# Checking decoded weights: half of the second reads replaced by bytes kept while decoding, one bitwise pass per check, and w_out's sums moved

## Chip, cores and metric

One core of a Trainium2 chip. The metric is the device time of one execution in microseconds; three executions of the kernel before were timed. [...]

## What is computed

Attention with 4 sink keys and a window of 128 keys, then a two-layer MLP with a leaky ReLU, in float32 precision:

```python
def _attn_ref(q, k, v, n_sink, window):          # q, k, v: 4 x 8 x 768 x 64
    scores = scale * np.matmul(q, k.transpose(0, 1, 3, 2))
    keep = is_sink | in_window
    scores = np.where(keep, scores, -1000000000.0)
    a = np.exp(scores - np.max(scores, axis=-1, keepdims=True))
    a = a / (np.sum(a, axis=-1, keepdims=True) + 1e-09)
    return np.matmul(a, v)
...
    x = attn_out.transpose(0, 2, 1, 3).reshape(B * S, H * D)     # 3072 x 512
    h = x @ w_in                                  # 512 x 2048
    g = np.maximum(0.01 * h, h)
    return g @ w_out                              # 2048 x 512
```

The two weights arrive as 64-bit floats (`wq`, 32 blocks of 128 x 512 values, 512 KB each: 16 of w_in, 16 of w_out). The kernel has a general path for inputs with unusual limits or with weights out of a range of magnitude; a flag, computed at the end, says whether it has to run.

## The kernel before

The 3072 tokens are cut into eight units of 384. Units 0 to 5 go through the MLP by plain steps: `plain_step` takes one of 16 column blocks fc of w_in, makes h on TensorE (`h_part`, L420), the leaky ReLU on ScalarE and VectorE (L975, L981), and splits g into a high and a low part, both fp32r (`high_low`: ScalarE's cast L907, POOL's subtraction L908); `outputs` multiplies them with w_out (L927). All products are made from high and low parts in three passes. The last two units are multiplied together by a scheme of seven half-size products (`SEVEN`): eight `pair_step`s q make h (products z, L748), then `seven_outputs` makes the output (products y, L1254), 56 steps k. Attention of the next unit runs between the MLP steps (`soft`, `gather`, `values`, L442 to L604); `gather` transposes softmax rows (L506, L508), stores them to DRAM (`kd`, L510) and reads them back rearranged (`pt`, L512).

Weights. During unit 0, `fetch_weight` (L279) reads one block into one of three 512 KB buffers, `load_weight` decodes the two 32-bit words on VectorE (L291, L293, L295), `round_weight` splits the result (ScalarE L308, POOL L309). Checks: each of the 32 blocks is read a second time, from unit 2 on, by `fetch_check` (L327), and `check_weights` takes the largest and smallest magnitude of the top words with two VectorE reduces (L335). `check_step` is called at six column blocks of units 2 to 5 (`CHECK_AT`), then in pair steps 4 to 6 and at every third k of `seven_outputs`. `needs_general` reduces the two results to flags.

The seven products need sums of weight blocks. `prepare` does it for w_in, `prepare_o` for w_out (POOL: two sums L647, four passes of `sums` L656, two low parts L666 in `split_sums`, behind ScalarE's hio cast L665; the results go to DRAM, `tfar`). `hio` uses the same buffer (number 2) as many of the re-read blocks. Seven of the eight `prepare_o` start at the steps in `PREPARE_O`, the last in the pair stage. `conversions` does the same for the tokens (loads of `xfar` L702, POOL sums L704, casts L711, low parts L712). In a pair step `add` puts sums on VectorE or POOL by hand, `t2` and `t3` among them; `make` splits the pair's arrays for the output (all of these have line L1005 in the profile). `fetch_ts` reads `tfar` back.

Order. On TensorE the order is written by hand. On the other engines and on SP, which issues the transfers, a scheduler sets it from the program's order and its own estimates; each engine then works strictly in that order. `anchor` and `latest` tie an instruction to a place.

## Time and profile before

| | us |
|---|---|
| median of three runs | 673.57 (673.37 to 676.27) |
| profiled execution | 674.25 |
| its span, first to last instruction | 672.5 |
| TensorE busy, matmuls | 654.2 (97%) |
| TensorE busy, weight loads | 576.5 (86%) |
| VectorE busy | 493.5 (73%) |
| ScalarE busy | 344.3 (51%) |
| POOL busy | 517.8 (77%) |

Busy shares are averages over stages with different limits: unit 0 up to about 122 us with all the decoding, plain steps up to about 538 us, pair steps up to about 604 us, outputs to the end. A stage is read from the waits that TensorE has in it. Matmul ends are modelled in the profile, so an idle time of TensorE in a row can be some tenths of a us short. PE is TensorE, PEld its weight loads, DVE VectorE, ACT ScalarE.

### The profile page before, as it was taken

What the parts mean: (1) busy time and instruction counts of PE and PEld (TensorE: products, weight loads), DVE (VectorE), ACT (ScalarE), POOL (GpSimd) and SP (SyncE); (2) the same over time, 40 slices, a digit from 0 to 9 for tenths busy, and PEclk for the clock granted to TensorE, in tenths of its full rate; (3) what the DMA queues carried; (4) which work ended last, traced back from release to release, by engine and by line L of the source; (5) the groups of instructions that cost most, each with busy time, mean ns of one, the idle gap of its engine ahead of it and who ended that gap; (6) DMA issues with size and microseconds to landing.
All of it is one profiled execution on the core that took longest, in us unless ns stands there. A gap on an engine that the chain in (4) does not pass through costs nothing.

```text
span 672.5 us, 13091 instructions
## 1 busy us (share of the span) xinstructions
PE 654.2 (97%) x3884; PEld 576.5 (86%) x3884; DVE 493.5 (73%) x1327; ACT 344.3 (51%) x884; POOL 517.8 (77%) x625
## 2 busy tenths in 40 slices
...
GB/s 233 190 180 239 236 182 201 128 223 141 239 195 211 222 179 248 209 238 219 142 263 233 228 201 222 243 233 268 161 217 167 373 299 340 323 356 263 329 396 73
DMA packets 105964, 155.42 MB, mean 231 GB/s; under 512 B 23328, under 2 KB 69152, under 8 KB 105888
## 3 DMA queue, kind: packets, MB, share of 16 engines
...
## 4 chain that ended last, share of the span: by engine, by line
PE 81%; DMA 6%; DVE 5%; POOL 3%; issue 2%; SPq 1%; ACT 1%; DVEq 0%; POOLq 0%; ACTq 0%
PE h L420 25%; PE o L927 24%; PE z L748 9%; PE y L1254 8%; PE acc L573 5%; PE s L447 5%; PE s L442 2%; PE t L483 1%; DMA kd<-kt 1%; DMA odd<-tfar 1%; DMA work<-xfar 1%; DMA tfar<-owg 1%; POOL work L704 1%; PE warm L403 1%; DMA woraw<-in_wq 1%
## 5 line engine op out<-in xcount | busy, mean ns | idle before, releaser
L908 POOL TENSOR_TENSOR gl<-gmem,gh 128x384 fp32r<-128x384 f32 x91 | 93.6, 1029 | 49.4 <-PE o L927 37.7
L420 PE MATMUL h<-xmem,even 128*128 128x384 f32 x576 | 119.4, 342 | 1.0 <-DVE gmem L981 1.0
L420 PE MATMUL h<-xmem,odd 128*128 128x384 f32 x576 | 117.2, 340 | 0.5 <-DVE gmem L981 0.5
L456 ACT ACTIVATE pk<-pk,negm 128x132 f32<-128x132 f32 (+1 forms) x192 | 81.5, 425 | 64.9 <-DVE negm L454 60.5
L927 PE MATMUL o<-woh,gh 128*128 128x512 f32 x288 | 114.5, 398 | 0.0
L927 PE MATMUL o<-wol,gh 128*128 128x512 f32 x288 | 114.3, 397 | 0.0
L420 PEld LDWEIGHTS h<-xmem,even 128*128 128x128 f32 x576 | 99.5, 188 | 6.2 <-issue 1.9
L420 PEld LDWEIGHTS h<-xmem,odd 128*128 128x128 f32 x576 | 99.5, 188 | 5.6 <-issue 1.7
L927 PE MATMUL o<-woh,gl 128*128 128x512 f32 x288 | 85.3, 397 | 0.0
L907 ACT CAST gh<-gmem 128x384 fp32r<-128x384 f32 x96 | 49.0, 510 | 51.9 <-PE o L927 28.8
L393 POOL TENSOR_TENSOR qksp<-qkraw,qksp 64x396 fp32r<-64x396 f32 (+1 forms) x48 | 57.6, 1201 | 21.8 <-issue 11.7
L981 DVE TENSOR_TENSOR gmem<-h,gmem 128x384 f32<-128x384 f32 x95 | 52.3, 551 | 26.9 <-ACT gmem L975 26.2
L975 ACT ACTIVATE gmem<-h 128x384 f32<-128x384 f32 x95 | 46.2, 487 | 45.2 <-PE h L420 39.6
L454 DVE CUSTOM_DVE_ANT_0 pk<-s,m 128x132 f32<-128x132 f32 (+1 forms) x192 | 59.2, 317 | 8.9 <-PE s L447 3.6
L927 PEld LDWEIGHTS o<-woh,gl 128*128 128x128 f32 x288 | 52.4, 188 | 11.6 <-issue 0.5
L846 DVE COPY_PREDICATED s<-tri,s 128x128 f32<-128x128 int8 x120 | 34.5, 289 | 36.3 <-PE s L447 35.3
L927 PEld LDWEIGHTS o<-woh,gh 128*128 128x128 f32 x288 | 54.1, 188 | 8.2 <-issue 1.0
L927 PEld LDWEIGHTS o<-wol,gh 128*128 128x128 f32 x288 | 54.2, 188 | 8.1 <-issue 1.0
L447 PEld LDWEIGHTS s<-qksp 128*128 128x128 f32 x288 | 52.9, 188 | 5.9 <-issue 0.4
L447 PE MATMUL s<-qksp 128*128 128x260 f32 (+1 forms) x288 | 56.3, 277 | 0.1
L395 POOL TENSOR_TENSOR qksp<-qkraw,qksp 128x384 fp32r<-128x384 f32 x48 | 50.7, 1057 | 3.7
L525 DVE TENSOR_TENSOR pt<-pt,held 128x256 f32<-128x256 f32 (+1 forms) x96 | 45.4, 477 | 10.9 <-DMA pt<-kd 10.6
(293 smaller groups left out, 1356.3 us busy)
## 6 DMA issues: line engine op xcount, KB each, us to landing
...
```

Source lines behind the costliest of these rows:

```text
L393: nc.gpsimd.tensor_tensor(out=sp[D:P, TU:TU + n], in0=raw[D:P, TU:TU + n], in1=sp[D:P, TU:TU + n].bitcast(F32), op=ALU.subtract)
L395: nc.gpsimd.tensor_tensor(out=sp[:, TU + n:2 * TU + n], in0=raw[:, 0:TU], in1=sp[:, 0:TU].bitcast(F32), op=ALU.subtract)
L420: nc.tensor.matmul(ph[:, 0:TU], lhsT=part_in(fc, cc, int(c == 2)), rhs=xl if c == 1 else xh, start=at == 0, stop=at == 3 * NCC - 1)
L447: nc.tensor.matmul(pss[0][:, 0:kn], lhsT=sp[:, off + j * P:off + (j + 1) * P], rhs=sp[:, TU + k0:TU + k0 + kn], start=c == 0, stop=c == 1)
L454: anchor[0] = nc.vector.tensor_tensor_reduce(out=w, in0=src, in1=mask, scale=-SCALE, scalar=3.0e38, op0=ALU.add, op1=ALU.min, accum_out=neg)
L456: latest["act"] = nc.scalar.activation(out=w, in_=w, func=AF.Exp, scale=-1.0, bias=neg, accum_out=sm)
L748: nc.tensor.matmul(dst[:, 0:TU], lhsT=w[:, int(c == 2), k * P:(k + 1) * P], rhs=x[int(c == 1)][:, k], start=start and k == 0 and c == 0, s ...
L907: latest["act"] = nc.scalar.copy(out=gh, in_=g)
L908: low = on.tensor_tensor(out=gl, in0=g, in1=gh.bitcast(F32), op=ALU.subtract)
L927: nc.tensor.matmul(acc, lhsT=(gl if c == 2 else gh)[:, t * P:(t + 1) * P], rhs=(wl if c == 1 else wh)[:, cols], start=f == 0 and c == 0, s ...
L981: anchor[0] = nc.vector.tensor_tensor(out=g, in0=ph[:, 0:TU], in1=g, op=ALU.max)
L1254: nc.tensor.matmul(parts[t], lhsT=a, rhs=side(p, q, int(c == 1)), start=q == 0 and c == 0 and (end or t != 1), stop=q == NQ - 1 and c == 2 ...
```

## The change

The check is no longer a pair of reduces. One VectorE pass compares the top bytes of a block with the constant 0x3C by exclusive-or and ors the differences into a tile `trap` (`note` on packed bytes, `note_raw` on the bytes of a raw block with a stride of eight); `needs_general` masks `trap` once. Of the 32 blocks

- 16 have their top bytes copied by ScalarE while they are decoded (`keep_tops`, L315 of the changed kernel); each four copies are stored to DRAM (`topfar`, 256 KB), and two loads in unit 5 bring them back, eight to a load, for 16 passes of 128 x 128;
- 15 (`REFETCHED`) are still read again, 11 in units 1 to 5 (`check_some`) and 4 at k = 7, 8, 15, 16, 23, 24 of `seven_outputs` (`check_late`), none in the pair steps;
- one, the last, is checked from its first read.

The last start of `PREPARE_O` (step 91) is gone, so the last two `prepare_o` start in the pair steps. The sums `t2` and `t3` of pair steps 3, 4 and 5 are on VectorE in place of POOL, and `make` gives POOL every second low part in place of two in three for n above 7 (8 parts fewer). The last w_out block's high and low parts use the same memory as two of the byte tiles.

```diff
...
@@ -54,10 +55,14 @@
 EARLY = (2, 11), (1, 19), (1, 33)
 ROUND = 3
 PREPARE = 19, 23, 35, 39, 51, 55, 67, 71
-PREPARE_O = 27, 43, 59, 75, 83, 87, 91
+PREPARE_O = 27, 43, 59, 75, 83, 87
 WARM = 17
-W_LO = 1.125 * 2.0 ** -15
-W_HI = 1.875 * 2.0 ** 16
+W_TOP = 0x3C
+W_TOPS = 0x3C3C3C3C
+W_SAME = 0x7C7C7C7C
+NTOP = 4
+INSIDE = 11
+REFETCHED = 4, 5, 6, 7, *range(9, 30, 2)
 NQ = NFC // 2
 CL = 6
 NWB = (NU - CL) // 2
...
@@ -279,6 +285,38 @@
             nc.sync.dma_start(out=raw.rearrange("p f t -> p (f t)"), in_=wq[nm == "o", fc])
         fetched[nm, fc] = raw
 
+    def note(tops):
+        with tc.issue_after(anchor[0].ins):
+            nc.vector.scalar_tensor_tensor(out=trap, in0=tops, scalar=W_TOPS, in1=trap, op0=ALU.bitwise_xor,
+                                           op1=ALU.bitwise_or)
+
+    def note_raw(raw):
+        top = raw.rearrange("p f t -> p (f t)").bitcast(U8).rearrange("p (f b) -> p f b", b=8)[:, :, 7]
+        seen = trap.bitcast(U8)
+        with tc.issue_after(anchor[0].ins):
+            nc.vector.scalar_tensor_tensor(out=seen, in0=top, scalar=W_TOP, in1=seen, op0=ALU.bitwise_xor,
+                                           op1=ALU.bitwise_or)
+
+    tops, ntops, unread = [None], [0], []
+
+    def keep_tops(n, raw):
+        if n in REFETCHED:
+            return
+        if n == 2 * NFC - 1:
+            note_raw(raw)
+            return
+        top = raw.rearrange("p f t -> p (f t)").bitcast(U8).rearrange("p (f b) -> p f b", b=8)[:, :, 7]
+        after = latest.get("act", anchor[0]).ins
+        b, i = divmod(ntops[0], NTOP)
+        ntops[0] += 1
+        if not i:
+            tops[0] = wpool.tile([P, NTOP, P], I32, tag=f"last{b % 2}", name=f"tops{b}")
+        with tc.issue_after(after):
+            nc.scalar.copy(out=tops[0][:, i].bitcast(U8), in_=top)
+        if i == NTOP - 1 or ntops[0] == 2 * NFC - 1 - len(REFETCHED):
+            with tc.issue_after(anchor[0].ins):
+                nc.sync.dma_start(out=topfar[:, NTOP * b:NTOP * b + i + 1], in_=tops[0][:, 0:i + 1])
+
     def load_weight():
         nm, fc = take("load")
         if at["fetch"] < at["load"]:
@@ -287,6 +325,7 @@
         top, low_ = raw[:, :, 1], raw[:, :, 0]
         w = small(f"w{nm}{fc}", at["load"] % 3 == 0)
         d = bank("d", f"d{nm}{fc}").bitcast(I32)
+        unread.append((at["load"] - 1, raw))
         with tc.issue_after(anchor[0].ins):
             nc.vector.tensor_scalar(out=d, in0=top, scalar1=3, scalar2=0x3FFFFFFF,
                                     op0=ALU.logical_shift_left, op1=ALU.bitwise_and)
@@ -303,8 +342,8 @@
             both = tile_in(fc).bitcast(F32R)
             hi, lo, w = both[:, :, 0], both[:, :, 1], w.rearrange("p (a x) -> p a x", a=2)
         else:
-            hi = wpool.tile([P, 512], F32R, name=f"w{nm}h{fc}")
-            lo = wpool.tile([P, 512], F32R, name=f"w{nm}l{fc}")
+            hi, lo = (wpool.tile([P, 512], F32R, tag=f"last{i}" if fc == NFC - 1 else f"w{nm}{n}{fc}",
+                                 name=f"w{nm}{n}{fc}") for i, n in enumerate("hl"))
         nc.scalar.copy(out=hi, in_=w)
         nc.gpsimd.tensor_tensor(out=lo, in0=w, in1=hi.bitcast(F32), op=ALU.subtract)
         wts[nm, fc] = (hi, lo)
@@ -315,26 +354,50 @@
 
     def round_weights():
         while at["round"] < at["load"]:
+            if at["round"] == len(weights) - 1:
+                keep_all_tops()
             round_weight()
 
-    def fetch_check(n):
-        k, fc = divmod(n, NFC)
-        raw = big([P, 512, 2], I32, f"craw{n}", n % 3 if len(past) > ENDS else 2)
-        flat = raw.rearrange("p f t -> p (f t)")
-        parts = 1
-        for i in range(parts):
-            cols = slice(i * 1024 // parts, (i + 1) * 1024 // parts)
-            nc.sync.dma_start(out=flat[:, cols], in_=wq[k, fc][:, cols])
-        checks.append((n, raw))
-
-    def check_weights():
-        n, raw = checks.pop(0)
-        top = raw[:, :, 1].bitcast(F32)
-        for side, op in ((wmax, ALU.max), (wmin, ALU.min)):
+    def keep_some_tops(n):
+        for _ in range(min(n, len(unread))):
+            keep_tops(*unread.pop(0))
+
+    def keep_all_tops():
+        keep_some_tops(len(unread))
+
+    jobs = [(weights[n],) for n in REFETCHED[:INSIDE]]
+    late_jobs = [weights[n] for n in REFETCHED[INSIDE:]]
+    jobs += [(n, min(2 * NTOP, 2 * NFC - 1 - len(REFETCHED) - n)) for n in range(0, 2 * NFC - 1 - len(REFETCHED), 2 * NTOP)]
+
+    def check_late():
+        if len(checks) == 2 or checks and not late_jobs:
+            f, (raw,) = checks.pop(0)
+            f(raw)
+        if late_jobs:
+            nm, fc = late_jobs.pop(0)
+            raw = big([P, 512, 2], I32, f"craw{nm}{fc}", len(late_jobs) % 2)
+            with tied():
+                nc.sync.dma_start(out=raw.rearrange("p f t -> p (f t)"), in_=wq[nm == "o", fc])
+            checks.append((note_raw, [raw]))
+
+    def check_some():
+        if checks:
+            f, parts = checks.pop(0)
+            for part in parts:
+                f(part)
+        elif jobs:
+            job = jobs.pop(0)
+            if len(job) == 1:
+                (nm, fc), = job
+                raw = big([P, 512, 2], I32, f"craw{nm}{fc}", 2)
+                checks.append((note_raw, [raw]))
+                dst, src = raw.rearrange("p f t -> p (f t)"), wq[nm == "o", fc]
+            else:
+                first, n = job
+                dst, src = big([P, 2 * NTOP, P], I32, f"tops_back{first}", 2)[:, 0:n], topfar[:, first:first + n]
+                checks.append((note, [dst[:, i] for i in range(n)]))
             with tc.issue_after(anchor[0].ins):
-                nc.vector.tensor_reduce(out=side[:, n:n + 1], in_=top, axis=AX.X, op=op, apply_absolute_value=True)
-
-
+                nc.sync.dma_start(out=dst, in_=src)
 
     def native(u):
         return u < NATU
...
@@ -980,15 +1036,15 @@
         else:
             anchor[0] = nc.vector.tensor_tensor(out=g, in0=ph[:, 0:TU], in1=g, op=ALU.max)
         queue.append(high_low(step, g, nc.vector if u and fc == NFC - 1 else nc.gpsimd))
+        keep_some_tops(1)
         yield
+        keep_all_tops()
         if step in PREPARE:
             preparing.append(prepare(PREPARE.index(step)))
         if step in PREPARE_O:
             preparing.append(prepare_o(PREPARE_O.index(step)))
-        if 1 < u and fc in CHECK_AT and u * NFC + fc < (CL - 1) * NFC + ENDS:
-            check_step(CHECK_AT[fc])
-        if u == CL - 1 and fc > ENDS + 1:
-            check_step()
+        if u and fc in CHECK_AT and (u, fc) < (CL - 1, 8):
+            check_some()
         prepare_more()
         bring_back(fc)
         if fc == NFC - 1:
@@ -1078,8 +1134,6 @@
                 make()
             if q == NQ - 1:
                 fetch_ts(i - 7)
-            if 3 < q < NQ - 1 and i in (1, 4):
-                check_step(2)
             if q:
                 prepare_more()
             next(o, None)
@@ -1151,14 +1205,14 @@
                 store("A12", (workspace(0) if q % 2 else workspace(2))[:, 1:3])
 
         def t2():
-            add("pool" if q > 2 else "dve", s2, s1, a, ALU.subtract)
+            add("dve" if q < NQ - 2 else "pool", s2, s1, a, ALU.subtract)
             if q < STORED:
                 store("S3", gmem[:, q % 2:q % 2 + 1])
                 if q % 2:
                     store("S1", workspace(0)[:, 3:4])
 
         def t3():
-            add("pool" if q > 2 else "dve", s4, b, s2, ALU.subtract)
+            add("dve" if q < NQ - 2 else "pool", s4, b, s2, ALU.subtract)
             if q < STORED:
                 store(*(("S2", one[:, 3:4]) if q % 2 else ("S1", workspace(2)[:, 3:5])))
 
@@ -1195,7 +1249,7 @@
         src = apart.pop((p, q)) if q < STORED else gs[q][name]
         hi, lo = (hl[n % len(hl)][:, i * TU:(i + 1) * TU] for i in range(2))
         do("act", nc.scalar.copy, out=hi, in_=src)
-        add("pool" if n % 3 and n > 7 or n in (1, 4) else "dve", lo, src, hi.bitcast(F32), ALU.subtract)
+        add("pool" if n % 2 and n > 7 or n in (1, 4) else "dve", lo, src, hi.bitcast(F32), ALU.subtract)
         fetch_arrays()
 
     def t_slot(j):
@@ -1279,10 +1333,10 @@
                     if at["item"] <= k + len(hl):
                         make()
                 fetch_ts(k)
-                if checks and 4 < k < 45 and (k % 3 == 0 or k == 43):
-                    check_step()
+                if k in (7, 8, 15, 16, 23, 24):
+                    check_late()
                 if k == 46:
-                    assert not checks and ready[0] == 2 * NFC, (len(checks), ready)
+                    assert not checks and not jobs and not late_jobs, (jobs, checks, late_jobs)
                     behind(NU * NFC - 3)
                 if k == 53:
                     behind(NU * NFC - 2)
...
...
+    with tc.issue_after(after.ins):
+        nc.vector.tensor_scalar(out=trap, in0=trap, scalar1=W_SAME, scalar2=None, op0=ALU.bitwise_and)
+    for i, (src, bound) in enumerate(((negm, DEEP), (trap, 0.0))):
         with tc.issue_after(after.ins):
-            nc.vector.tensor_reduce(out=deep, in_=src, axis=AX.X, op=side)
-        nc.vector.tensor_scalar(out=bad[:, 3 + i:4 + i], in0=deep, scalar1=bound, scalar2=None, op0=op)
+            nc.vector.tensor_reduce(out=deep, in_=src, axis=AX.X, op=ALU.max)
+        nc.vector.tensor_scalar(out=bad[:, 3 + i:4 + i], in0=deep, scalar1=bound, scalar2=None, op0=ALU.is_gt)
...
```

Lines in the changed kernel are some 40 to 70 higher: L454 is L517 there, L907 L970, L975 L1031, L981 L1037, L656 L719, L666 L729, L704 L767, L712 L775, L1005 L1061.

ScalarE in unit 0, from the h of column block 3 to the cast of w_in's next block: first before (gh is the high part of g, wi and wo decoded blocks), then now (tops is the byte tile, wiraw a raw block).

```order
L975 ACTIVATE gmem<-h_3_760 128x384
L907 CAST gh_790<-gmem 128x384
L308 CAST odd_106<-wi_680 128x2x256
L456 ACTIVATE pk_1_2_804,sm_1_627<-pk_1_2_804,negm 128x260 x2
L554 CAST st_0_845<-sk_0_839 128x128
L555 COPY r_0_844<-sk_0_839 128x384
L975 ACTIVATE gmem<-h_4_832 128x384
L308 CAST woh_714<-wo_687 128x512
L907 CAST gh_864<-gmem 128x384
L308 CAST even<-wi_748 128x2x256
```

```order
L1031 ACTIVATE gmem<-h_3_769 128x384
L970 CAST gh_799<-gmem 128x384
L315 COPY tops_730<-wiraw_755 128x512
L347 CAST odd_106<-wi_687 128x2x256
L519 ACTIVATE pk_1_2_814,sm_1_634<-pk_1_2_814,negm 128x260 x2
L617 CAST st_0_855<-sk_0_849 128x128
L618 COPY r_0_854<-sk_0_849 128x384
L1031 ACTIVATE gmem<-h_4_842 128x384
L347 CAST woh_721<-wo_694 128x512
L970 CAST gh_874<-gmem 128x384
L315 COPY tops_730<-wiraw_828 128x512
L347 CAST even<-wi_757 128x2x256
```

Two of the byte copies stand there now, each directly behind a gh cast and ahead of a weight's cast and, for the first, of two exponentials.

POOL in unit 5, ahead of the first pair step (owf and owg are the sums of w_out blocks, work the token sums), before and now:

```order
L712 TENSOR_TENSOR even<-work_6345,even 128x384
L656 TENSOR_TENSOR owf_6567<-owg_6568,owf_6567 128x256
L908 TENSOR_TENSOR gl_6661<-gmem,gh_6660 128x384
L656 TENSOR_TENSOR owg_6568<-owg_6568,owf_6567 128x256
L656 TENSOR_TENSOR owg_6568<-owg_6568 128x256
L666 TENSOR_TENSOR owf_6567<-owf_6567,hio_6666 128x512
L908 TENSOR_TENSOR gl_6696<-gmem,gh_6695 128x384
L666 TENSOR_TENSOR owg_6568<-owg_6568,hio_6666 128x512
L704 TENSOR_TENSOR work_6345<-work_6346,work_6345 128x384
L704 TENSOR_TENSOR work_6346<-work_6346,work_6345 128x384
```

```order
L971 TENSOR_TENSOR gl_6597<-gmem,gh_6596 128x384
L971 TENSOR_TENSOR gl_6660<-gmem,gh_6659 128x384
L767 TENSOR_TENSOR work_6384<-work_6384 128x384
L775 TENSOR_TENSOR even<-work_6384,even 128x384
L971 TENSOR_TENSOR gl_6690<-gmem,gh_6689 128x384
L971 TENSOR_TENSOR gl_6720<-gmem,gh_6719 128x384
L767 TENSOR_TENSOR work_6384<-work_6385,work_6384 128x384
L767 TENSOR_TENSOR work_6385<-work_6385,work_6384 128x384
```

The four passes L656 (three are shown) and two L666 of the seventh `prepare_o` are gone from between the low parts of g and the token sums; they come 8 to 20 rows later, behind the first sums of the pair steps.

VectorE in unit 5, at the transposes of the last head pair (kt is what goes to DRAM as kd, pt what comes back), before and now:

```order
L858 RECIPROCAL held<-held 128x3
L859 TENSOR_TENSOR pk_7_6367<-pk_7_6367,held 128x396
L981 TENSOR_TENSOR gmem<-h_9_6447,gmem 128x384
L335 TENSOR_REDUCE wmax<-craw_6408 128x1
L335 TENSOR_REDUCE wmin<-craw_6408 128x1
L506 STREAM_TRANSPOSE kt_3_1_6454<-pk_7_6367 128x4x96
L712 TENSOR_TENSOR even<-work_6345,even 128x384
L508 STREAM_TRANSPOSE kt_3_1_6454<-sk_118 128x4x32
L981 TENSOR_TENSOR gmem<-h_10_6506,gmem 128x384
L525 TENSOR_TENSOR pt_3_6424<-pt_3_6424,held 128x4x96
```

```order
L921 RECIPROCAL held<-held 128x3
L922 TENSOR_TENSOR pk_7_6406<-pk_7_6406,held 128x396
L569 STREAM_TRANSPOSE kt_3_1_6491<-pk_7_6406 128x4x96
L1037 TENSOR_TENSOR gmem<-h_9_6484,gmem 128x384
L775 TENSOR_TENSOR even<-work_6384,even 128x384
L571 STREAM_TRANSPOSE kt_3_1_6491<-sk_119 128x4x32
L1037 TENSOR_TENSOR gmem<-h_10_6541,gmem 128x384
L588 TENSOR_TENSOR pt_3_6461<-pt_3_6461,held 128x4x96
```

The check of a re-read block stood between the softmax's last scaling and its transpose; it is gone from there.

## Rows read from the trace of the kernel before

**Rows 1.** The page: busy time by engine, and the chain that ended last, by engine.
```profile
PE 654.2 (97%) x3884; PEld 576.5 (86%) x3884; DVE 493.5 (73%) x1327; ACT 344.3 (51%) x884; POOL 517.8 (77%) x625
...
PE 81%; DMA 6%; DVE 5%; POOL 3%; issue 2%; SPq 1%; ACT 1%; DVEq 0%; POOLq 0%; ACTq 0%
```

**Rows 2.** Busy us of PE, PEld, DVE, ACT, POOL by stretch; clock, DMA share, GB/s.
```profile
30.00:60.00 30.00, 28.61 (x169) 22.18 (x169) 27.88 (x64) 20.19 (x53) 20.97 (x35) 1.00 0.59 191
...
590.00:620.00 30.00, 29.43 (x206) 28.89 (x206) 28.18 (x36) 15.25 (x33) 28.54 (x25) 1.00 0.91 322
```

**Rows 3.** TensorE's waits: line, releaser, us in total, times, longest.
```profile
PE acc L569 <- DVE st L532: 1.7, 1, 1.7
PE z L748 <- ACT work L1005: 1.6, 1, 1.6
PE h L420 <- DVE gmem L981: 1.5, 2, 1.0
PE y L1254 <- DMA odd<-tfar: 1.1, 1, 1.1
PE z L748 <- POOL even L712: 1.1, 1, 1.1
PE acc L573 <- DVE pt L525: 0.9, 2, 0.5
PE y L1254 <- DVE xmem L1005: 0.6, 1, 0.6
```

**Rows 4.** The tile craw: its transfers, and one of those that waited for it.
```profile
L327 SPq DMA_DIRECT2D craw<-in_wq x32: 327/333/707, 215.1 to 650.6; - x32
...
  ACT hio L665: 1.6, 1
```

**Rows 5.** VectorE by line and shape, 500 to 665 us: busy us, mean ns.
```profile
L335 DVE TENSOR_REDUCE wmax<-craw 128x1 f32<-128x512 f32 x22 | 14.9, 676 | 5.4 <-DMA craw<-in_wq 5.4
...
L1005 DVE TENSOR_TENSOR xmem<-last_v,xmem 128x384 fp32r<-128x384 f32 x1 | 1.4, 1366 | 0.0
...
L1005 DVE TENSOR_TENSOR xmem<-gmem,xmem 128x384 fp32r<-128x384 f32 x1 | 0.6, 569 | 1.5 <-ACT xmem L1005 1.5
```

**Rows 6.** VectorE by line, 0 to 120 us: the decode.
```profile
L293 DVE SCALAR_TENSOR_TENSOR di<-wiraw,di 128x512 int32<-128x512 int32 x16 | 11.1, 694 | 0.3
```

**Rows 7.** VectorE in order of time, 500 to 522 us: start, us, [idle before].
```profile
507.50 0.69 DVE L335 TENSOR_REDUCE wmax<-craw 128x1 f32<-128x512 f32 x1 [2.94 <-DMA craw<-in_wq]
...
517.67 0.56 DVE L525 TENSOR_TENSOR pt<-pt,held 128x384 f32<-128x384 f32 x1 [6.97 <-DMA pt<-kd]
```

**Rows 8.** SP in order of time, issues of weight fetches: start, us.
```profile
54.63 0.33 SPq L279 DMA_DIRECT2D wiraw<-in_wq  x1
...
500.99 0.38 SPq L327 DMA_DIRECT2D craw<-in_wq  x1
```

**Rows 9.** The chain that ends at 545 us: start, us, what.
```profile
500.46 5.77 DMA work<-xfar
...
510.37 3.87 DMA kd<-kt
```

**Rows 10.** POOL in order of time, 519 to 543 us.
```profile
526.37 1.30 POOL L647 TENSOR_TENSOR owf<-woh,wol 128x512 f32<-128x512 f32 x1 [2.94 <-DMA tfar<-owg]
...
541.48 0.99 POOL L712 TENSOR_TENSOR even<-work,even 128x384 fp32r<-128x384 f32 x1
```

**Rows 11.** The chain that ends at 640 us.
```profile
608.62 1.30 DVE xmem L1005
...
630.14 6.05 DMA odd<-tfar
```

**Rows 12.** ScalarE by line, 0 to 125 us.
```profile
L308 ACT CAST woh<-wo 128x512 fp32r<-128x512 f32 x16 | 9.9, 620 | 7.7 <-DVE wo L295 7.6
```

**Rows 13.** The weight fetches of L279, 40 to 120 us.
```profile
DMA to landing us min/median/max: 3.4/3.7/5.1
```

**Rows 14.** ScalarE in order of time, 46 to 68 us.
```profile
57.54 0.62 ACT L308 CAST even<-wi 128x512 fp32r<-128x512 f32 x1 [0.62 <-DVE wi L295]
```

27 lines of the change are left out of this document (11 added, 16 removed).

## The prediction

> **What bounds the kernel now.** I read the busy line and the chain first [rows 1]. [...] The change takes no matmul away, so the only time it can give back is time in which TensorE stands still, and the only time it can cost is a new standstill. So the second view is the list of TensorE's own waits [rows 3]. Five of its entries are late in the program and have names that the change touches: 1.7 + 0.9 us in the last pooled-key products (L569, L573, through VectorE), 1.1 us in the first pair products (L748 behind POOL's L712), 1.6 us in the fifth pair step (L748 behind ScalarE's copy) and 1.1 us in the output products (L1254 behind a transfer of tfar). With 0.6 us behind VectorE's last_pt and xmem they make 7.0 us. That is the ceiling of what can be won late. 0.5% of the kernel is 3.4 us, about what a measurement of this kernel can tell from no change, so the forecast hangs on whether half of that ceiling goes.
>
> The profiled execution took 674.25 us (span 672.5); the median of the three runs is 673.57, 0.7 us less. I make the sum on the profiled one and take the difference off the median.
>
> **What goes, by busy time.** The change removes 32 transfers of 512 KB and their 64 reduces [rows 4, 5]. 22 checks, that is 44 reduces of 676 ns and 29.7 us of VectorE, lie after 500 us [rows 5]. In their place stand 15 transfers, one 128x512 bitwise pass each, one such pass on the last w_out weight, 4 stores of 256 KB, 2 loads of 512 KB and 16 passes of 128x128. The bitwise pass is not in the trace. Its nearest row is the decode's SCALAR_TENSOR_TENSOR of the same 512 elements, 694 ns [rows 6]. The pass has two inputs from SBUF, though, and additions of that kind, one shape, spread from 569 to 1366 ns [rows 5], so its ends are 0.69 and 0.69 + 0.80 = 1.49 us; I take 0.69, since the row has the same length and kind of operation. The passes of 128 elements lie below it. After 500 us only four long ones remain, 2.8 to 6.0 us for 29.7. None of this is a gain by itself; it is worth what it frees of the stalls below.
>
> [...]
>
> **Stall A, 517 to 521 us, 2.6 us.** VectorE sits idle 2.94 us for a re-read weight at 507.50 [rows 7]; its transfer was issued at 500.99 [rows 8]. Then come two reduces (1.35 us), and only then the transposes whose store kd is waited for. That transfer takes 3.87 us from 510.37, and before it the chain has 5.77 us of work<-xfar, which started at 500.46, beside the re-read [rows 9]. VectorE then waits 6.97 us for pt<-kd at 517.67 [rows 7]. In the changed order the check is gone, so the big transpose goes some 4 us earlier. What is late next is the small transpose (L508): it waits for POOL, and POOL for work<-xfar. If that transfer takes as long as now, next to nothing is left of the gain; if it is shorter without the 512 KB beside it, most is. Ends: 0 and 2.6. I take 1.3, the middle, since the chain names the transfer and the idle row the re-read, and neither rules the other out.
>
> **Stall B, 541 us, 1.1 us.** POOL reaches L712 at 541.48 without any idle time ahead; its queue is late because w_out's seventh sum waits 2.94 us for tfar at 526.37 and then puts four passes L656 and two L666 ahead of L704 [rows 10]. The changed order has all eight of these pieces behind the pair stage's first adds. The 1.1 us goes whole. What is charged instead: these 8 us, and those of the eighth sum, stand between the adds of pair steps 1 to 4. TensorE has no wait on POOL there now, so I cost it at nothing; the cover is POOL's slack in the pair stage, and rival 2 has the price if it is gone.
>
> **Stall C, 585 us, 1.6 us.** ScalarE's hio cast waits 1.6 us for a check, since both use one buffer [rows 4]; ScalarE's copy of z stands behind the cast, and TensorE behind the copy [rows 3]. The changed pair stage re-reads no weight. The 1.6 us goes whole.
>
> **Stall D, 609 us, 0.6 us.** Here VectorE is simply full: 28.18 of 30 us at 590 to 620 [rows 2], and the last add on the chain takes 1.30 us at 608.62 [rows 11]. Two checks ahead of it (four reduces, 2.7 us) go, but the two adds t2 and t3 of the fifth pair come onto VectorE. A two-input add of 128x384 takes from 0.57 to 1.37 us there [rows 5], so 1.1 to 2.7 us come. I take 0; ends -0.6 and +1.0, the latter because TensorE arrives some 3 us earlier than now while VectorE's work is as long.
>
> **Stall E, 635 us, 1.1 us.** odd<-tfar, 256 KB, takes 6.05 us from 630.14 [rows 11], where kd's 256 KB took 3.87 [rows 9]. Re-reads run beside it up to 650.6 [rows 4]; afterwards the last four are issued before it. At 3.87 us the stall is gone, at 6.05 it stays: 0 to -1.1, and I take -0.9, nearer the uncrowded row.
>
> **Stage one, a cost.** ScalarE now also copies 16 times 128x512. Its nearest row is the cast of that shape, 620 ns [rows 12], 9.9 us in all. A copy stands right behind a gh cast and waits for its weight to land, with all later ScalarE work behind it. One case: the fetch at 54.63 [rows 8] lands after 3.4 to 5.1 us, median 3.7 [rows 13], that is 58.3; ScalarE is ready at 57.54 - 0.62 = 56.92 [rows 14]. So 1.4 us of waiting, of which the 0.62 us of idleness at 57.54 covers part, and the VectorE pass that needs the exponentials behind it is late by the rest. VectorE is busy 27.88 of 30 us here and can't make up much [rows 2]. TensorE waits little here now: 1.5 us in two places of the whole program for L981, which follows ScalarE [rows 3]. Most copies are covered by ScalarE's idle third (20.19 of 30 us busy). I take +0.9 us; ends 0 (all covered) and +2.5 (two such waits pass to TensorE). A store queues on SP behind its fourth copy and weight fetches queue behind the store; they can't start before the same copies have freed their buffers, so I cost this at nothing beyond the 0.9. The last weight's high part also waits for such a store to leave its tile; it is issued late enough that I cost nothing.
>
> Between 125 and 500 us TensorE has next to no standstill and VectorE gets lighter: 0. The end of the program is the same but for one pass on the trap tile in place of a reduce: 0.
>
> **Sum:** -1.3 - 1.1 - 1.6 + 0 - 0.9 + 0.9 = -4.0 us, so 670.2 on the profiled execution and **669.6** on the median, 0.6% faster.
>
> **Rivals.**
> 1. *Only the queue stalls go.* A and E are latencies of transfers that stay (kd, pt, xfar, tfar); the re-reads may not be what makes them long. Against: the 2.94 us at 507.50 names the re-read. For: a stall that goes early makes everything later arrive at the same transfers sooner. Then -1.1 - 1.6 + 0.9 = -1.8, 671.8 us, not to be told from no change. Chance 0.2.
> 2. *VectorE and POOL take the pair stage.* The reduces that go take 676 ns on the mean where both engines are busy; the additions that come spread from 569 to 1366 ns [rows 5]. If the moved ones run at the upper end, the six of pairs 3 to 5 cost 8.2 us of VectorE for the six checks (8.1 us) removed nearby, and in pair 3 nothing goes: 2.7 us come onto an engine near full. Stall C is then given back: -4.0 + 1.6 = -2.4, 671.2 us; with 1 us of D 672. Take 672. Against: over 500 to 665 us VectorE loses 29.7 us and gets at most 6.0 + 14 x 1.37 = 25.2. [...] Chance 0.12.
> 3. *ScalarE makes stage one late, slower.* If the landing waits go through to TensorE at most of the 16 copies: half of the 9.9 us of copies and two landing waits of 1.4 us uncovered, 7.8 us, against 4.9 won late: +2.9, and with A and E not won +5.1, so some 677 us. It decides when a copy's wait exceeds the idle time that ScalarE has next behind it, like the 0.62 us at 57.54 [rows 14]. Against: ScalarE is one third idle there. For: VectorE, which waits for it, is not. Chance 0.07.
> 4. *The edit doesn't do what it says:* a byte read with a stride of eight costs far more than its neighbours; at double the price, 0.69 us more on each of four late passes (-4.0 + 2.8 = -1.2, 672.4) and 0.62 on each copy, which takes stage one from +0.9 to its end of +2.5 (674.0). Chance 0.04.
>
> **How the numbers follow.** The forecast has 0.57: 666 to 670.1, faster by over 0.5%. Rivals 1, 2 and most of 4 are within 0.5%, with 0.35; slower has 0.08 (rival 3 and the tail of 4). The best sum is -2.6 - 1.1 - 1.6 - 0.6 - 1.1 + 0 = -7.0, 666.6; the worst of the forecast's own ends, 0 - 1.1 - 1.6 + 1.0 - 0 + 2.5 = +0.8, 674.4. The range is 666.0 to 674.5.
>
> **What would show it.** Right: no VectorE idle for a re-read near 507; L712's last pass on POOL a microsecond earlier relative to TensorE; no wait of hio for a check; the tfar transfer at 630 in 4 to 5 us; TensorE's list of waits shorter by about five us late and longer by one early. Wrong: TensorE's waits before 125 us grown by over 3 us behind gmem or sm; new waits at L748 behind VectorE in pair steps 3 to 6; odd<-tfar still at 6 us.

## The result and the profile after

The changed kernel takes 680.89 us (median of 4), the kernel before 673.95 in the same set: a ratio of 1.0102 [1.0070, 1.0135], slower by about 1%. The forecast was 669.6, faster. The profiled execution took 680.36 us, its span of 678.6 is 6.1 us longer than before, at a granted clock of 1.00, full speed in the profile's count, in the stretches that the argument uses.

TensorE's own waits in the profile after (line, releaser, us in total, times, longest) answer to [rows 3]; lines are 54 to 63 higher (L748 is L811, L1254 L1308):

```profile
PE s L510 <- DVE negm L517: 3.2, 3, 1.3
PE z L811 <- ACT work L1061: 3.1, 3, 1.5
PE y L1308 <- DMA even<-tfar: 2.5, 1, 2.5
PE h L483 <- DVE gmem L1037: 1.9, 2, 1.4
PE y L1308 <- DVE xmem L1061: 1.4, 1, 1.4
...
PE acc L632 <- DVE negm L517: 1.0, 1, 1.0
PE acc L636 <- DVE pt L588: 0.9, 2, 0.5
```

What the prediction called stalls A and B is gone or shorter: no wait of the pooled products for st, none of z for POOL. Stall C has not gone but grown from 1.6 to 3.1 us over three places, E from 1.1 to 2.5, D from 0.6 to 1.4. New is the first row: the score products wait 3.2 us for VectorE's negm, in the plain steps, for which the prediction had charged nothing.

The account below takes, for each place, the distance between the starts of two neighbouring matmuls beyond what is usual for that pair of operands; it is the same reading for every run below. The first column has the times of the places; the columns before and after are read from one execution each.

| place, us | before | after | difference | predicted |
|---|---|---|---|---|
| unit 0 (first h of unit 1) | at 123.55 | at 124.28 | +0.7 | +0.9 |
| 219 and 222 | 0 | 1.11 + 1.43 | +2.5 | 0 |
| 404 and 452 | 0.51 | 1.25 | +0.7 | 0 |
| 487 to 491 | 0.49 | 1.13 | +0.6 | 0 |
| A, 517 to 523 | 3.15 | 1.19 | -2.0 | -1.3 |
| B, 541 | 1.23 | 0 | -1.2 | -1.1 |
| C, 561, 566, 588 | 1.71 | 0.93 + 0.98 + 1.66 | +1.9 | -1.6 |
| D, 609 to 613 | 0.73 | 1.59 | +0.9 | 0 |
| E, 635 to 638 | 1.27 | 2.63 | +1.4 | -0.9 |

The sum is +5.5 of the 6.1; the rest lies in gaps of under 0.4 us each.

How far one execution can be trusted shows in e4, e5 and e6 (below), which have the changed kernel's order of work up to 560 us. At 452 us they have 0.56, 1.42 and 2.38 us for its 1.25, at 491 us 1.1 each as it has. At stall A TensorE's waits for st and pt are 0.5, 2.2 and 1.9 us for its 0.9, where the kernel before and two with its checks (e7, e8) have 2.4 to 2.6. So 491 is steady, 452 is there every time at another size, and what is won at A goes from 0.4 to 2.1 us with the execution.

**Why 452.** VectorE in order of time there (start, us, what, [idle before and releaser]). The softmax of the next scores needs COPY_PREDICATED, L517 and L920 to L922 in this order; passes over the kept bytes (L290) stand between them:

```profile
447.06 0.28 DVE L290 SCALAR_TENSOR_TENSOR trap<-tops_back,trap 128x128 int32<-128x128 int32 x1
447.26 0.29 DVE L517 CUSTOM_DVE_ANT_0 pk<-s,m 128x132 f32<-128x132 f32 x1
...
447.47 3.07 DVE L290 SCALAR_TENSOR_TENSOR trap<-tops_back,trap 128x128 int32<-128x128 int32 x3
450.46 0.15 DVE L920 TENSOR_SCALAR held<-sm 128x3 f32<-128x3 f32 x1
450.57 1.05 DVE L290 SCALAR_TENSOR_TENSOR trap<-tops_back,trap 128x128 int32<-128x128 int32 x1
```

One such pass takes 0.28 us, and three of the same shape take 3.07. The longest, 1.38 us from 449.16, starts 0.1 us behind a POOL subtraction of 1.33 us (L456, 449.06) and ends just behind it. By line and shape over the whole span (busy us, mean ns), the passes over kept bytes and over re-read blocks:

```profile
L297 DVE SCALAR_TENSOR_TENSOR trap<-crawo,trap 128x512 uint8<-128x512 uint8 x13 | 12.1, 932 | 5.1 <-DMA crawo<-in_wq 5.1
L290 DVE SCALAR_TENSOR_TENSOR trap<-tops_back,trap 128x128 int32<-128x128 int32 x16 | 9.4, 589 | 0.1
```

The reduces of 676 ns [rows 5] took 665 to 687 every time; the new long pass has a mean of 932, the short one of 589. Over the whole span the 32 passes take 24.9 us where the 64 reduces took 43.2, but between 120 and 500 us 20.2 stand where 13.5 stood. VectorE's busy time is still what it was (493.9 us for 493.5 [rows 1]), since the moved additions fill what the checks gave back after 500 us: without them (e9) it is 480.1, and the additions alone (e8) make it 505.0.

**Why 561 to 588.** ScalarE's hio casts of the two w_out sums that stand in the pair stage (the moved seventh and the eighth, which stood there before):

```profile
561.08 0.62 ACT L728 CAST hio<-owf 128x512 fp32r<-128x512 f32 x1 [3.34 <-POOL owf L719]
566.40 0.62 ACT L728 CAST hio<-owg 128x512 fp32r<-128x512 f32 x1 [1.31 <-POOL owg L719]
584.12 0.62 ACT L728 CAST hio<-owf 128x512 fp32r<-128x512 f32 x1 [2.14 <-POOL owf L719]
588.78 0.62 ACT L728 CAST hio<-owg 128x512 fp32r<-128x512 f32 x1 [3.66 <-POOL owg L719]
```

The copies of z that TensorE needs stand in ScalarE's queue behind a cast that waits for POOL: the next instruction that reads z starts 0.52 to 0.53 us behind the start of each of the four, at 561.61, 566.92, 584.64 and 589.31 us. Busy us of PE, PEld, DVE, ACT and POOL, clock, DMA share and GB/s at 560 to 580, before and after:

```profile
560.00:580.00 20.00, 20.00 (x116) 20.00 (x115) 18.57 (x30) 5.32 (x11) 16.69 (x16) 1.00 1.01 355
```

```profile
560.00:580.00 20.00, 18.41 (x103) 17.77 (x102) 17.22 (x23) 5.88 (x12) 19.21 (x17) 1.00 1.02 346
```

POOL, with 16.69 of 20 us before, has 19.21 now. Two things of the change meet here, and the other profiles part them. The standstills at 561 and 566 (0.8 to 1.0 us each) are in all profiles without checks in the pair stage but e6, also where the seventh sum stands ahead of it (e1, e9 to e11, best3 to best6), and in none with checks there (before, e7, e8, best2). The one at 588 (1.5 to 1.8 us; 3.3 in e5 and e6) is in those that have the seventh sum in the pair stage and no checks there: after, e2, e3b, e4, e5, e6, e12. In e7 and e8, as before, that place belongs to the check.

**Why 638.** SP in order of time (start, us), then VectorE:

```profile
632.22 2.23 SPq L380 DMA_DIRECT2D crawo<-in_wq  x2
634.51 0.91 SPq L1061 DMA_DIRECT2D even<-tfar  x2
```

```profile
630.69 1.50 DVE L297 SCALAR_TENSOR_TENSOR trap<-crawo,trap 128x512 uint8<-128x512 uint8 x1 [0.87 <-DMA crawo<-in_wq]
633.41 0.68 DVE L297 SCALAR_TENSOR_TENSOR trap<-crawo,trap 128x512 uint8<-128x512 uint8 x1
```

The late re-reads have two buffers. The first issue stands on SP until the pass of 1.50 us has freed one, at 632.2, the second until 634.1; both tfar loads that TensorE is about to need stand behind them. They are the price that the forecast left out at E: SP waiting for VectorE. The late loads are a condition of this standstill, since it is gone without them (e4), but not all of it: e7 and e8, with the late re-reads of the kernel before, have 3.0 and 3.2 us there, and what lengthens it in them was not followed.

### The profile page after: what moved, and what is told of

Read it like the earlier page. It is cut to its first block, busy times and chain, and to the rows that moved or that the text cites. A ratio compares the mean times of both kernels' runs of the same rounds, so it can differ in the third digit from the quotient of the medians.

```text
span 678.6 us, 13055 instructions
## 1 busy us (share of the span) xinstructions
PE 654.5 (96%) x3884; PEld 575.5 (85%) x3884; DVE 493.9 (73%) x1308; ACT 353.0 (52%) x900; POOL 510.0 (75%) x612
## 4 chain that ended last, share of the span: by engine, by line
PE 78%; DVE 6%; DMA 5%; POOL 5%; issue 3%; ACT 1%; SPq 1%; DVEq 0%; ACTq 0%; POOLq 0%
PE o L990 27%; PE h L483 27%; PE y L1308 8%; PE acc L636 6%; PE s L510 4%; PE z L811 2%; PE s L505 1%; DMA qkn<-in_qp 1%; DVE trap L290 1%; PE t L546 1%; DMA even<-tfar 1%; DMA ring_pt<-far 1%; POOL work L1061 1%; DMA tfar<-owf 1%; POOL owg L710 1%
## 5 line engine op out<-in xcount | busy, mean ns | idle before, releaser
L456 POOL TENSOR_TENSOR qksp<-qkraw,qksp 64x396 fp32r<-64x396 f32 (+1 forms) x48 | 57.3, 1194 | 23.1 <-issue 12.9
L970 ACT CAST gh<-gmem 128x384 fp32r<-128x384 f32 x96 | 49.2, 512 | 48.1 <-PE o L990 27.1
L1037 DVE TENSOR_TENSOR gmem<-h,gmem 128x384 f32<-128x384 f32 x95 | 52.3, 551 | 27.4 <-ACT gmem L1031 26.4
L1031 ACT ACTIVATE gmem<-h 128x384 f32<-128x384 f32 x95 | 46.2, 486 | 43.5 <-PE h L483 38.2
L517 DVE CUSTOM_DVE_ANT_0 pk<-s,m 128x132 f32<-128x132 f32 (+1 forms) x192 | 59.2, 317 | 8.7 <-PE s L510 4.0
L455 ACT CAST qksp<-qkraw 128x780 fp32r<-128x780 f32 (+1 forms) x48 | 43.1, 897 | 14.9 <-PE s L510 12.3
```

The source lines that it names most:

```text
L456: nc.gpsimd.tensor_tensor(out=sp[D:P, TU:TU + n], in0=raw[D:P, TU:TU + n], in1=sp[D:P, TU:TU + n].bitcast(F32), op=ALU.subtract)
L517: anchor[0] = nc.vector.tensor_tensor_reduce(out=w, in0=src, in1=mask, scale=-SCALE, scalar=3.0e38, op0=ALU.add, op1=ALU.min, accum_out=neg)
L970: latest["act"] = nc.scalar.copy(out=gh, in_=g)
L1031: nc.scalar.mul(g, ph[:, 0:TU], 0.01)
L1037: anchor[0] = nc.vector.tensor_tensor(out=g, in0=ph[:, 0:TU], in1=g, op=ALU.max)
```

## The experiments

Each ratio is to the kernel before, run beside it. The changed kernel stands at 1.0102 [1.0070, 1.0135]. Of the runs that change one thing in it, e1 and e4 are apart from it by their times; the intervals of e2, e3b, e5 and e6 overlap with its own, and there the trace has to decide.

**Are the passes dear because of their two inputs?** e3_reduce_tops, then e3b_reduce_tops:

```diff
-            nc.vector.scalar_tensor_tensor(out=trap, in0=tops, scalar=W_TOPS, in1=trap, op0=ALU.bitwise_xor,
-                                           op1=ALU.bitwise_or)
+            nc.vector.tensor_reduce(out=deepest[0], in_=tops.bitcast(F32), axis=AX.X, op=ALU.max)
```

> The changed kernel with the 16 passes over the kept bytes made by a reduce, which has one SBUF input in place of two, at the same places in the same order (the kept bytes go unchecked). Port theory (a pass with two SBUF inputs and a POOL instruction wait for each other): the passes take 250 to 300 ns each in place of 250 to 1381, the standstill of 1.25 us at 452 us goes and that at 491 us falls from 1.1 to about 0.5: about 679.1 us. Rival (eight passes in a row are late whatever they are): 680.3 to 681 us, with passes as short but the standstills there.

It gave nothing: its reduce wrote into trap itself, the flag was raised and the general path ran, 4885 us. The second one has a tile of its own:

> The changed kernel with its sixteen 128x128 passes over the kept bytes turned into one-input maximum reduces into a tile of their own (the loads, their order and their number of elements per partition stay; the kept top bytes of 17 weights are read but not checked). Theory A, the passes are dear because they have two SBUF inputs and take turns with POOL: they took 250 to 1381 ns, 589 on the mean; as reduces they take 250 to 350 ns every time, TensorE's standstill at 452 us (1.25 us) goes and the one at 491 (1.13 us) shrinks to about 0.5; the ones at 218 and 222 us and those after 555 us stay. Some 2 us less than the changed kernel: 678.9 us, ratio to the kernel before 1.0075. Theory B, the standstills come from the queue places and the loads of the checks, whatever the pass is: all stay, 680.9 us, ratio 1.010.

Measured 678.46, 1.0065 [1.0034, 1.0096]. The sixteen reduces:

```profile
L290 DVE TENSOR_REDUCE deepest<-tops_back 128x1 f32<-128x128 f32 x16 | 4.5, 279 | 0.1
```

279 ns for 589, and the standstills at 452 and 491 are both gone (2.4 us). They are gone in the three other profiles with these reduces too (e10 to e12) and stand in all seven with the changed kernel's passes (after, e1, e2, e4, e5, e6, e9): theory A. In the profile after, eight passes took 604 to 1381 ns: seven start while a POOL instruction has 0.46 us or more to go, one at the same moment as a POOL instruction (487.73), and all eight end 0.14 to 0.15 us behind its end (the longest at 450.54, POOL's at 450.39). The eight others, 250 to 292 ns, start with none running, ahead of one, or 0.06 us before one ends. The reduces of the kernel before stay at 665 to 687 ns, though 56 of the 64 run beside a POOL instruction. So VectorE was the one held up here, in the softmax chain.

**The late re-reads.** e4_no_late:

```diff
-    late_jobs = [weights[n] for n in REFETCHED[INSIDE:]]
+    late_jobs = []
```

> The changed kernel without the four late re-reads and their checks in the output stage (four of the 32 blocks go unchecked). SP theory (the re-reads stand ahead of the tfar loads in SP's queue and delay them): the standstill of 2.6 us at 638 us falls to 1 or less, about 679 us. Rival (VectorE and POOL run full from 605 to 630 us, the low parts are late, and with them the loads behind them): 2 us or more stay, 680.3 to 681 us.

Measured 678.4, 1.0035 [1.0012, 1.0059]: the standstill at 638 is gone, the one at 612 stays at 1.59. The SP theory, and D is not the late checks' doing.

**The checks in unit 1.** e2_from_unit2:

```diff
-    jobs = [(weights[n],) for n in REFETCHED[:INSIDE]]
+    jobs = [(weights[n],) for n in REFETCHED[3:INSIDE]]
...
-        if u and fc in CHECK_AT and (u, fc) < (CL - 1, 8):
+        if u > 1 and fc in CHECK_AT and (u, fc) < (CL - 1, 8):
```

> The changed kernel without its three re-reads and checks in unit 1 (three of the 32 blocks go unchecked; nothing else is left out). Queue theory (the note at 178 us holds VectorE 1.7 us for its transfer and the one at 194 us 1.6 us beside POOL, and what they delay comes out at TensorE at 219 and 222 us): the two standstills of together 2.5 us shrink to the 0.3 us of the kernel before, about 678.6 us. Rival (unit 1 is late because stage one ended 0.7 us late, or because the store of tfar is slow): the standstills stay, 680.5 to 681 us.

Measured 679.1, 1.008 [1.0045, 1.0115]; 219 and 222 are both gone in its trace. That looked like a proof, and later runs took it back. Two kernels below, e7 and e8, carry out the kernel before without any difference up to about 500 us, and both show, at 200 to 240 us, the wait that the first profile of it lacks (e7's row):

```profile
PE s L447 <- DVE negm L454: 1.3, 1, 1.3
```

So the 1.4 us at 222 come and go between executions of one and the same order of work, and belong to no part of the change. What decides them can be read. A multiplication on VectorE with two SBUF inputs (st) stands ahead of negm, and a subtraction on POOL (qksp) starts at almost the same moment. POOL's row and VectorE's (start, us), before, then after:

```profile
219.72 1.73 POOL L393 TENSOR_TENSOR qksp<-qkraw,qksp 64x524 fp32r<-64x524 f32 x1 [2.81 <-issue]
219.72 0.55 DVE L532 TENSOR_TENSOR st<-pt,own 128x384 fp32r<-128x384 f32 x1
```

```profile
221.78 1.30 POOL L456 TENSOR_TENSOR qksp<-qkraw,qksp 64x524 fp32r<-64x524 f32 x1 [4.01 <-issue]
222.00 1.50 DVE L595 TENSOR_TENSOR st<-pt,own 128x384 fp32r<-128x384 f32 x1
```

Where the two start within 0.03 us of each other (before, e2, best3), st takes 0.55 us, POOL 1.69 to 1.73, and TensorE stands still for nothing. Where POOL starts 0.09 to 0.24 us earlier (the fifteen others but best4, which has a check there), POOL takes 1.30, st 1.49 to 1.62, and TensorE's 1.4 us are there. The 1.1 at 219 may belong to the checks in unit 1: 0.5 to 1.1 us stand there in seven of the eight profiles that have them, and in one (e12, 0.58) of the seven other profiles of changed kernels.

**The moved sums and additions.** Of the three moved things (sums, additions, checks), five kernels have other subsets. From the changed kernel, e1_sums_back has the first hunk, e5_adds_back the two others (and t3 like t2), e9_checks_only all; from the kernel before, e7_only_sums and e8_only_adds make the same two edits the other way round:

```diff
-PREPARE_O = 27, 43, 59, 75, 83, 87
+PREPARE_O = 27, 43, 59, 75, 83, 87, 91
...
-            add("dve" if q < NQ - 2 else "pool", s2, s1, a, ALU.subtract)
+            add("pool" if q > 2 else "dve", s2, s1, a, ALU.subtract)
...
-        add("pool" if n % 2 and n > 7 or n in (1, 4) else "dve", lo, src, hi.bitcast(F32), ALU.subtract)
+        add("pool" if n % 3 and n > 7 or n in (1, 4) else "dve", lo, src, hi.bitcast(F32), ALU.subtract)
```

> The changed kernel with the seventh w_out sum started at step 91 again, so that one sum and not two lie in the pair steps. Queue theory (the hio casts of the moved sums wait for POOL on ScalarE, and the copies of z wait behind them): of TensorE's three standstills behind ScalarE's copies in the pair steps (0.9, 1.0 and 1.7 us at 561, 566 and 588 us) at least two go, and the 1.2 us behind POOL's L775 at about 545 us come back: 680.9 - 2.4 = about 678.5 us. Rival (POOL has 8 us more or less to do wherever the sum stands): what is won in the pair steps is lost ahead of them, 680 to 681 us.

> The changed kernel with the additions where the kernel before has them: t2 and t3 of pairs 3 to 5 on POOL, and POOL's share of the high/low remainders one in three as before. Theory A, the standstill at 613 us (1.59 us) is VectorE being full with moved additions: it falls to the 0.7 us that the kernel before has there, and TensorE's wait for xmem goes; the ones at 561, 566 and 588 us (behind ScalarE's casts that wait for POOL) grow a little, since POOL has more to do. About 0.9 us less than the changed kernel: 680.0 us, ratio 1.0088. Theory B, POOL is what the pair stage waits for once the two w_out sums stand there: giving it additions back makes 561 to 590 longer by more than 613 gains, and the time is 681 to 683 us, ratio 1.011 to 1.013.

> The kernel before with one thing of the change: w_out's seventh sum moved into the pair stage. Theory A, the move by itself is dear, because the pair stage's POOL is full at 560 to 580 us and ScalarE's casts wait for its sums with the copies of z behind them: the standstill at 541 us goes (1.2 us), two new ones of about 1 us appear near 560 to 570 and the one at 585 grows to 3 us or more: 676 us, ratio 1.003 or above. Theory B (the prediction's), POOL has slack there: 541 goes and nothing comes, 672.7 us, ratio 0.998.

> The changed kernel with the seventh sum and all additions where the kernel before has them, so that only the checks differ from the kernel before. Theory A, the exchange of the checks alone costs 218, 222, 452 and 491 us (4.4 us of standstill) and the one at 637 (2.6 us), gains 2 us at 517 to 521 and the 1.6 us at 585: about 3 us slower than the kernel before, 678.5 us, ratio 1.0045. Theory B, most of the loss comes from the sums and the additions in the pair stage: ratio 1.000 to 1.002.

> The kernel before with one thing of the change: t2 and t3 of pairs 3 to 5 and a part of the high/low remainders on VectorE in place of POOL or the other way round, as the change has them. Theory A, POOL is the fuller engine of the pair stage, and the additions are the part of the change that helps: the standstill at 609 us goes to 0.7 or less and those at 541 and 585 stay: 673 to 675 us, ratio 0.996 to 1.000. Theory B, with the checks of the kernel before still on VectorE there is no room: 677 us or more, ratio 1.002.

| new in it | median, us | ratio |
|---|---|---|
| sums alone (e7) | 684.41 | 1.0128 [1.0093, 1.0162] |
| additions alone (e8) | 677.31 | 1.0041 [1.0021, 1.0060] |
| checks alone (e9) | 680.94 | 1.0091 [1.0058, 1.0123] |
| checks, additions (e1) | 677.43 | 1.0030 [1.0013, 1.0046] |
| checks, sums (e5) | 685.43 | 1.0131 [1.0084, 1.0179] |
| all three (the change) | 680.89 | 1.0102 [1.0070, 1.0135] |

Each of the three alone makes the kernel slower: theory A for e7, though not at the places that it names, theory B for e5 and e8, and e9 loses more than its theory A said. POOL had no slack for the sums. In e7 the standstill at 541 shrinks (1.23 to 0.47), as predicted, and three larger ones stand behind it: 1.83 at 603, 2.19 at 612, 3.02 at 641; 3.7 us of its output products' waits are for POOL. With the checks changed, the additions on VectorE help (e1 against e9), but they are no gain by themselves: e8 has 3.17 us at 635. e1 is faster than its queue theory said, but not as it said: 588 alone of the three is gone, and 541 is not back. In e5 giving POOL its additions back leaves 613's kind at 1.60 and makes 588's kind 3.28, so D's growth isn't VectorE being full of moved additions. Taking the checks out of the pair stage is enough for it: best3 (below), the kernel before with its checks moved in time, has 1.37 us there for 0.73, as have e1 and e9 to e11, and the kernels with the seventh sum in the pair stage as well have 1.60 (after, e2 to e5, e12). But the moved additions alone bring 1.46 too (e8), and why is open.

**Is it ScalarE's queue, or POOL?** e6_pool_cast:

```diff
-                nc.scalar.copy(out=hi, in_=src)
+                (nc.gpsimd.tensor_copy if q in ("o6", "o7") else nc.scalar.copy)(out=hi, in_=src)
```

> The changed kernel with one thing else: the high-part casts of the two w_out sums that stand in the pair stage are done by POOL, right behind the sums that POOL makes, and no longer by ScalarE. Theory A, the standstills at 561, 566 and 588 us (0.93 + 0.98 + 1.66 us) come from ScalarE's queue: a cast waits up to 3.7 us for POOL's sum, and the copies of z that TensorE needs stand behind it. Then all three go, about 3 us less than the changed kernel: 677.9 us, ratio 1.006. Theory B, POOL's own work is the bound there and ScalarE's wait only shows it: the standstills move to VectorE's and POOL's products and the time stays within 0.7 us of the changed kernel, 680 to 682 us, ratio 1.009 to 1.012.

Measured 680.29, 1.0078 [1.0046, 1.0109]. 561, 566 and 588 are gone and one standstill of 3.28 us stands at 595. The same stretch of it:

```profile
560.00:580.00 20.00, 19.77 (x113) 19.45 (x112) 17.01 (x21) 4.75 (x10) 20.00 (x18) 1.00 1.03 381
```

POOL never pauses, and the time fits theory B: ScalarE's wait only showed where POOL is the bound. The run isn't a clean test, though: its four casts take 0.94 us each on POOL and so add 3.8 us to the engine that it finds full. A kernel with ScalarE's copies of z ahead of those casts was not run.

**Do the causes add up?** e10_all_four is e2, e3b, e4 and e1 in one:

> The changed kernel with the four things undone at once that the single runs gave a price: no checks in the second unit, no late re-reads (together 7 weights unread a second time), the passes over the kept bytes as one-input reduces (17 weights unchecked), the seventh w_out sum before the pair stage. Theory A, the four are separate causes and add up: 2.4 + 2.6 + 2.4 + 1.7 = 9.1 us less than the changed kernel, 671.8 us, ratio 0.997; what of the change is left is then a gain of 2 us over the kernel before. Theory B, they hide behind each other: 675 us or more, ratio 1.000 or above.

Measured 671.95, 0.9945 [0.9925, 0.9965], where 671.8 was expected: theory A, and 3.6 us faster than the kernel before, with 23 of the 32 blocks not looked at (7 re-reads and the 16 with kept bytes; the last is still checked, so the 17 of the expectation is one too many). That the time is hit is in part luck: the 2.4 us for the checks in unit 1 hold the 1.4 at 222, which this run still has, and by the ratio to its own kernel before, where 0.997 was expected, the four gave back 10.6 us rather than 9.1. Its waits have no tfar any more, and z's have halved:

```profile
PE z L811 <- ACT work L1061: 1.5, 2, 0.8
PE s L510 <- DVE negm L517: 1.3, 1, 1.3
```

Two more runs start from it. e12_sums_in leaves PREPARE_O as the changed kernel has it; e11_no_copies has this:

```diff
-        with tc.issue_after(after):
-            nc.scalar.copy(out=tops[0][:, i].bitcast(U8), in_=top)
...
+            nc.vector.memset(tops[0], 0)
```

> The run that undid four things with only three undone: w_out's seventh sum stands in the pair stage again, as in the changed kernel. Theory A, the sum's price there is the 1.7 us of the standstill at 588 us and no more: 673.7 us, ratio 0.997. Theory B, it is more, 3 us as the pair of timed runs (1.0102 and 1.003) would have it, since the work behind it on POOL and ScalarE is late too: 675.5 us, ratio 1.000. Theory C, the prediction's, it gains the 0.8 us at 542: 671 us, ratio 0.993.

Measured 673.5, 0.9972 [0.9955, 0.9988]: 1.6 us more, and 1.77 us stand at 585. Theory A.

> The run that undid four things, with ScalarE's sixteen copies of the top bytes left out too (the kept bytes are then zeros from a fill by VectorE, and nothing is checked on them; stores and loads stay). Theory A, the copies make stage one 0.3 to 0.9 us late, and that lateness is what turns into the standstill of 1.44 us near 222 us, a place decided within a microsecond: TensorE's 384th product of the second unit comes 0.5 us earlier, the standstill at 222 goes, 1.5 to 2 us less: 670 us, ratio 0.992. Theory B, the copies are covered and the standstill near 222 has another cause: no difference, 672 us, ratio 0.9945.

Measured 675.82, 0.9991 [0.9970, 1.0012], slower than e10, not faster; the standstill near 222 stays. From the first h of unit 0 to the first of unit 1 it takes 102.8 us, in e10 103.0, in the changed kernel 102.6 and before 102.0. Over all profiles it is 101.6 to 102.3 in the four without byte work in unit 0 (before, e7, e8, best3) and 102.1 to 103.4 in the fourteen with the copies, some 0.6 us more on the mean. Leaving the copies out thus gave nothing that stands out of the spread, but VectorE's four fills of 128 x 512, which the run has instead, may hide what the copies cost: whose the 0.6 us are is open. Of the 3 us that its profile is longer than e10's, 1.8 stand at 521 and 522, stall A once more; why the run is slower on the median is open too.

**Versions with every weight checked.** best2 and best3 were the first tries. best2 has e5's edit and the seventh sum of e1, checks only from unit 2 on, the kept bytes in four loads, later places for the last three re-reads, and this:

```diff
-            if q:
+            if q and i == 0:
                 prepare_more()
+            if 2 < q < NQ - 1 and i in (1, 4):
+                check_late(2, 3)
```

> A version meant to lose what the runs so far put a price on, with every weight still checked. Against the changed kernel: checks only from the third unit on (2.4 us less, by the run without checks in the second unit); in the pair stage only one w_out sum in place of two, and paced at one slice per half step (the run with one sum back lost the standstill at 588 us); additions on POOL as in the kernel before; six re-reads spread over the third to sixth pair step and three that are fetched well behind the last tfar loads (the run without late re-reads lost the standstill at 637 us, 2.6 us). Theory A, the standstills have separate causes and add up: 2.4 + 1.7 + 0.9 + 2.6 = 7.6 us less than the changed kernel, 673.3 us, ratio 0.999; less the 1.2 us of a returned standstill at 541 us, 674.5. Theory B, removing one lets the next limit show (VectorE and POOL together are full): no more than half comes, 677 us, ratio 1.005.

Measured 680.15, 1.0069 [1.0044, 1.0093]. 561, 566 and 638 are gone, but four standstills of 0.5 to 1.6 us stand at 607 to 616 behind VectorE: theory B. best3 is the kernel before with this:

```diff
-CHECK_AT = {4: 1, 5: 0, 8: 1, 9: 0, 12: 1, 13: 0}
+CHECK_AT = {4: 1, 5: 1, 6: 0, 8: 1, 9: 1, 10: 0, 12: 1, 13: 0}
...
-        if u == CL - 1 and fc > ENDS + 1:
-            check_step()
...
-            if 3 < q < NQ - 1 and i in (1, 4):
-                check_step(2)
```

> The kernel before with its own checks (maximum and minimum reduces) moved only in time, all 32 weights checked: five in place of three per unit from the third unit on, none at 500 to 520 us and none in the pair stage, the last thirteen in the output stage as before. Theory A, the prediction's readings of stall A (a re-read ahead of the transposes, 2.6 us of which the changed kernel won 2.0) and of stall C (a check that holds the buffer of the eighth sum, 1.6 us) are right, and reduces do no harm among the units because they have one input: 3 us less than the kernel before, 672.5 us by this set's runs of it, ratio 0.9955. Theory B, VectorE can't take two more reduces a check in the units, or the eighth sum without the check to hold it starts earlier and meets POOL full at 560 us: 0.999 to 1.005.

Measured 682.46, 1.0105 [1.0081, 1.0130]. That is slower than even theory B had it. For stall C it is the nearest to a clean test, with sums and additions unmoved: without the check 585 is gone, and 0.82 and 0.96 us stand at 567 and 572 in its place. At 520 there are 6.28 us; the chain to there runs through a work<-xfar transfer and POOL's sums, and why was not followed further.

best4 is e1's edit with the check in one-input forms (for re-reads the two reduces of the kernel before) and `CHECK_AT = 0, 1, 4, 5, 8, 9, 12, 13` from unit 2 on, its last three re-reads late in `seven_outputs`.

> A version with every weight checked, built on the run that undid four things: w_out's seventh sum before the pair stage; re-read weights by a maximum and a minimum reduce as in the kernel before; the kept bytes by one tensor_scalar in place and one maximum reduce for each eight weights; no check in the second unit, four in place of three in each later unit (twelve re-reads and two loads of kept bytes before 490 us), none in the pair stage, and three re-reads fetched near 645 us, behind the last transfers that the products wait for. Theory A, the gain of the four is kept because what does the checks disturbs nobody: at most 1 us above the run that left 24 checks out, so 672 to 673 us, ratio 0.995 to 0.997. Theory B, a large part of that run's gain was the work left out, and twelve pairs of reduces among the units make VectorE late: 675 us or more, ratio at or above 1.000.

Measured 690.33, 1.0221 [1.0194, 1.0248]: theory B and beyond. Steady as they are, reduces still take their time, 1.35 us a check at a place where VectorE had it not (4.3 us of standstill at 220, where VectorE also idles 1.77 us for the block itself, and 1.4 to 2.0 at 309, 394, 413, 479 and 500).

best5 and best6 keep the changed kernel's passes over re-read blocks; best5 keeps their places among the units too, and both have e1's edit:

```diff
-            nc.vector.scalar_tensor_tensor(out=trap, in0=tops, scalar=W_TOPS, in1=trap, op0=ALU.bitwise_xor,
-                                           op1=ALU.bitwise_or)
+            nc.vector.tensor_scalar(out=tops, in0=tops, scalar1=W_TOPS, scalar2=W_SAME, op0=ALU.bitwise_xor,
+                                    op1=ALU.bitwise_and)
...
+            nc.vector.tensor_reduce(out=keptmax[:, nkept[0]:nkept[0] + 1], in_=tops, axis=AX.X, op=ALU.max)
...
-                if k in (7, 8, 15, 16, 23, 24):
-                    check_late()
+                if k in (34, 39, 43, 44, 45):
+                    check_late(3)
```

best6 adds INSIDE = 8, e2's condition and k in (7, 34, 35, 36, 40, 43, 44, 45).

> The changed kernel with three things else, every weight checked: w_out's seventh sum before the pair stage; the kept bytes by one tensor_scalar in place and one maximum reduce for each eight weights in place of sixteen passes with two inputs; the last four re-reads fetched behind the last tfar transfer that the products wait for (three near 648 us, one a few us on). The checks in the units stay at the places of the changed kernel, three a unit from the second unit on. Theory A, the three are separate causes and number and place of the checks were what best4 lost by: 671.95 us of the run with four things undone, plus 1.5 us for the checks in the second unit: 673.5 us, ratio 0.997. Theory B, the gain of that run was work left out: 675.5 us or more, ratio 1.000 or above.

> best5 with no check in the second unit: eight re-reads in the later units, and seven in the output stage, three of them fetched near 607 us and looked at near 648 us, the others fetched behind that. Theory A as for best5, without its 1.5 us: 672 us, ratio 0.9945. Theory B, three transfers of 512 KB near 607 us delay the tfar loads that stand behind them, and TensorE has a standstill of 1 to 2.5 us near 612 to 637: 674 us or more, ratio above 0.997.

Measured 674.51, 0.9985 [0.9966, 1.0005], between best5's two theories, and 674.54, 0.9975 [0.9955, 0.9995], best6's theory B by the number but not by its reason: at 612 to 637 us its trace has no more than best5's. Both beat the changed kernel clearly. best6 beats the kernel before by about 0.25%, less than the 0.5% that the prediction took as tellable, though its interval leaves 1 out. At least half of e10's gain is thus gone once every weight is checked. Two passes of best5 and their reduces (us, mean ns):

```profile
L293 DVE TENSOR_REDUCE keptmax<-tops_back 128x1 f32<-128x1024 int32 x2 | 2.4, 1204 | 0.0
...
L290 DVE TENSOR_SCALAR tops_back<-tops_back 128x1024 int32<-128x1024 int32 x2 | 2.0, 986 | 0.0
```

The first pair takes 1.9 us at 445, and TensorE doesn't stand still; the second takes 2.5 us at 485 to 489, around two multiplications, one of 1.21, and 1.8 us of standstill stand at 488.

## Why the prediction was wrong, step by step

The sum was -4.0 us, and the profiles differ by +6.1. Four terms failed in their mechanism: nothing charged for the moved sum, C, E, and nothing charged among the plain steps.

- *Stall A, -1.3, taken as the middle of 0 and 2.6:* right in kind, -2.0 measured. VectorE idles there for a product of TensorE (4.46 us at 519.78), no longer for pt. The size is luck: by TensorE's waits for st and pt the changed kernel's profile wins 1.7 of the 2.6, and e4, e5 and e6, with the same order of work there, 2.1, 0.4 and 0.7, nearly both ends of the prediction's range.
- *Stall B, -1.1:* right, -1.2.
- *"What is charged instead: these 8 us ... I cost it at nothing; the cover is POOL's slack":* failed. It is the step that turned the gain of B into a loss: in the changed kernel the sum costs the 1.66 us at 588, e12 has its price at 1.6 us with the other causes gone, and e7 at up to 9 us without the moved additions. The number to read was POOL's 16.69 of 20 us at 560 to 580, where 8 us more don't fit.
- *Stall C, "The 1.6 us goes whole":* failed. The check was not only a wait, it also held the eighth sum's casts back to 585; without it they come at 560 to 572 and wait for POOL's sums, and two standstills are in its place (1.8 us in best3, 1.9 in e9 and after). Taking the check away by itself won nothing here.
- *Stall D, 0:* +0.9. It lies within the upper end of +1.0, but neither late checks (e4) nor moved additions (e5) make it; taking the checks out of the pair stage is enough (best3, 1.37 us).
- *Stall E, -0.9, "nearer the uncrowded row":* failed, +1.4. The prediction looked at the length of a transfer; the wait was on SP, for a buffer, with the loads queued behind, and without the late re-reads it is gone (e4).
- *Stage one, +0.9:* the size is right, +0.7, and +0.6 on the mean of all profiles; the cause given, ScalarE's copies, is not shown, since the run without them has fills in their place and is no shorter (e11).
- *"Between 125 and 500 us ... VectorE gets lighter: 0":* failed, and it rests on the price of a pass. "I take 0.69" for passes of 512 bytes, with those of 128 elements "below it": 932 and 589 ns on the mean were measured, and the 1.49 that [rows 5] had given as the upper end was reached and passed (1.56). The short passes alone put 2.4 us at 452 and 491, where 1.0 stood before at 404 and 487. The price of two inputs came out at VectorE, where eight of the short passes lasted until 0.15 us behind the end of a POOL instruction.

The rival that came nearest is the second, VectorE and POOL together, but at another place and dearer; the third had the right sign and a mechanism, ScalarE in stage one, that at most 0.6 us bear out. The measured 680.89 lies 6.5 us above the worst sum of the prediction's own ends.
